# Threshold attention and a squared-ReLU layer: last keys padded with zeros, exponentials head by head, values between two parts of turning

## The chip, the cores and the metric

The kernel runs on one core of one Trainium2 chip. The metric is the device time of one execution in microseconds (us). A core has TensorE (PE), which multiplies matrices into PSUM, VectorE (DVE), ScalarE (ACT), GpSimd (POOL) and SyncE (SP, which here only issues DMAs). Each engine works through a queue of its own; semaphores order the engines among one another.

## The reference

Eight batches of eight heads attend over 576 tokens of 64 values. A score counts only if it lies within tau of its row's maximum. The result is laid out as 4608 tokens by 512 and goes through two matrix products with a squared ReLU between them.

```python
scores = scale * np.matmul(q, k.transpose(0, 1, 3, 2))      # scale = 1/8
thresh = np.max(scores, axis=-1, keepdims=True) - tau
scores = np.where(scores >= thresh, scores, -1000000000.0)
scores = scores - np.max(scores, axis=-1, keepdims=True)
attn = np.exp(scores)
attn = attn / (np.sum(attn, axis=-1, keepdims=True) + 1e-09)
attn_out = np.matmul(attn, v)                               # 8, 8, 576, 64
x = attn_out.transpose(0, 2, 1, 3).reshape(4608, 512)
h = x @ w_in                                                # 512 -> 2048
r = np.maximum(h, 0.0)
out = (r * r) @ w_out                                       # 2048 -> 512
```

Here q, k, v and the output are float32; the two weights come as float64, and the kernel rounds them to float32.

## The kernel before

**Visits and steps.** The kernel takes two heads at a time: a visit is one pair of heads with some of its blocks of 128 queries. 576 is four blocks of 128 and a rest of 64; the rests of the two heads make one block of 128 rows (block 4, the single-head block, since it needs one tile of scores in place of two). Visits 0 to 3 hold blocks 0 and 1 of the first batch's four pairs, visits 4 to 7 the blocks 2 to 4 of the same pairs, later visits all five. A step is one block of one visit. Steps 0 to 34 are visits 0 to 10, which turn the weights on PE ("early" below, though the kernel's own `early()` is true for steps 0 to 9 alone). From step 35 on (`by_dma`) DVE transposes 32x32 blocks and DMAs place them through DRAM. From visit 12 on (`paired`, `late_step`) visits go two by two.

**One early step** (the loop at L1082): `round_weights` stage 0, `scores` (L253: one PE product for each head and half of the keys, into banks 0 to 3; L268), `maxima` (L305, DVE), `turn(old, 0)` and `turn(old, 1)` for the block of two steps ago (L381: three PE transposes each, L388 for the single-head block; ACT copies them to `wT`, L382, L390), `exponents` (L314: on ACT the bias -max/8 at L317, the threshold max - 8 tau at L318, for both heads at once, then one exponential for each head, L320), `fill` with pieces of the MLP, `mix` (L493: the values of the block three steps ago, L496), its copy to `xT` (`put`, L479), `turn(old, 2)`, `threshold` (L323: DVE masks by comparing scores with the threshold and sums, L332, L334, L335), and `divide` (L337, POOL).

**Banks.** `take("tx", (4, 5))` deals PSUM banks 4 and 5 out in turn to the parts of turning and to the values; `take("mm", (6, 7))` deals 6 and 7 to MLP pieces, and to part 1 of turning while `early()` is true. A bank given out again waits until ACT has copied what it held.

**Rounding of weights.** The weights are rounded to float32 in 32 portions: stage 0 on ACT (L149, L150), 1 and 2 on DVE (L152, L154), 3 and 4 on POOL (L156, L158). Steps 2, 4 and 6 take one portion each, steps 8 to 33 one each, and steps 15, 18 and 22 two. Portion p + 3 is loaded after portion p is done.

**MLP pieces.** A piece is 8 or 4 products. `rate` spreads those at hand over the steps; each step has four calls of `fill`. Pieces are mlp_in (L544), mlp_out (L726) in the first chunk of 256 tokens, and from the third chunk on the seven-product scheme (L655, L761).

**The last keys.** `wT` holds the turned weights with keys on partitions. Keys 512 to 575 of head 0 lie on its partitions 0 to 63 and those of head 1 on 64 to 127, of one shared column block. In late visits the queries of the second group (`TWO`) have the two heads the other way round. The last keys' values are therefore loaded onto both halves of `vs`, and `mix` closes with products of 64 rows (`above`, `below`). `turn_blocks` (L406) writes each block's rest columns in one transpose for blocks 0 and 1 (L427), in two for blocks 2 and 3 (L429, L430).

**Order.** All five queues are in the order of the program (`manual_schedule`); nothing reorders them. `prep` (L227) transposes q and k of the next visit on DVE (L242) in a visit's last step.

Of the kernel before, what the change touches and what calls it, by code (L numbers as in the profile page):

```python
# [19 lines left out]
def kernel(  # L20
# [182 lines left out]
    def arrived(t):  # L203
        assert all(x[0].tensor.name != t.tensor.name for x in loads)

    def load_v(n):
        b, h = divmod(visits[n][0], HP)
        h *= 2
        t = vs[n % 2]
        if paired(n):  # L210
            both = t.rearrange("p (u c) d -> p u c d", u=2)
            src = v[b, h:h + 2]
            for u in range(2):
                loads.append((both[:, u, 0:NBLK, :], src[u, 0:NBLK * P, :].rearrange("(c p) d -> p c d", p=P)))
            for half in range(2):
                loads.append((both[half * D:(half + 1) * D, :, NBLK, :], src[:, NBLK * P:S, :].rearrange("u p d -> p u d")))
            return
        todo = []
        for u in range(2):
            at = u * (NBLK + 1)  # L220
            todo.append((t[:, at:at + NBLK, :], v[b, h + u, 0:NBLK * P, :].rearrange("(c p) d -> p c d", p=P)))
            for half in range(2):
                todo.append((t[half * D:(half + 1) * D, at + NBLK, :], v[b, h + u, NBLK * P:S, :]))
        for to, src in todo:
            nc.sync.dma_start(out=to, in_=src)

    def prep(n):  # L227

        prep_part(q, n)
        prep_part(k, n)  # L230
# [83 lines left out]
    def exponents(vis, i):  # L314
        w, sc, st = weights[vis, i]
        mx, thr, bias = (st[:, j, 0:len(sc)] for j in range(3))
        nc.scalar.activation(out=bias, in_=mx, func=AF.Copy, scale=-SCALE)  # L317
        nc.scalar.activation(out=thr, in_=mx, func=AF.Identity, bias=ntau8)  # L318
        for u in range(len(sc)):
            nc.scalar.activation(out=w[:, u, :].rearrange("p (h k) -> p h k", h=2), in_=sc[u],  # L320
                                 func=AF.Exp, bias=bias[:, u:u + 1], scale=SCALE)
# [84 lines left out]
    def turn_blocks(vis, i):  # L406
# [13 lines left out]
        if two:  # L420
            wb = wb[:, :, :, i % 2, :]
            whole_, rest_ = (w[:, :, x0 * 32:x1 * 32].rearrange("p u (c j q) -> p u c j q", q=32, j=n)
                             for x0, x1, n in ((0, M, 4), (M, KB, 2)))
            h = M // 4
            move(wb[:, 0:h, :, :], whole_[:, 0, :, :, :])  # L425
            if i < 2:
                move(wb[:, h, :, :].rearrange("p (u j) q -> p u j q", u=2), rest_[:, :, 0, :, :])  # L427
            else:
                move(wb[:, h, 2:4, :], rest_[:, 0, 0, :, :])  # L429
                move(wb[:, h, 0:2, :], rest_[:, 1, 0, :, :])  # L430
            move(wb[:, h + 1:, :, :], whole_[:, 1, :, :, :])  # L431
            return
        parts = [(0, 0, KB, 0), (1, M, KB, KB), (1, 0, M, KB + 2)] if paired(vis) else [(0, 0, KB, 2), (0, M, KB, 0)]
# [58 lines left out]

    def mix(n, cols):  # L493

        def term(ps, u, c, at, rows=slice(0, P), first=False, last=False):
            nc.tensor.matmul(ps[u * D:(u + 1) * D, :], vs[n % 2][rows, u * (NBLK + 1) + c, :],  # L496
                             wT[rows, at // REST:(at + ps.shape[1]) // REST, NBLK if c == NBLK else u * (NBLK + 1) + c, :],
                             start=first, stop=last)

        above, below = slice(0, D), slice(D, P)  # L500
        arrived(vs[n % 2])
        if not by_dma(n):
            ps = take("tx", (4, 5))[:, 0:cols.stop - cols.start]
            for c in range(NBLK):
                for u in range(2):
                    term(ps, u, c, cols.start, first=(c == 0))
            for u, rows in enumerate((above, below)):
                term(ps, u, NBLK, cols.start, rows, last=True)
            put(n, cols.start, ps, False)
            return  # L510
        n1, n2 = 2 * P + REST, 2 * P
        at = ODD if paired(n) and n % 2 else ONE
        one, two = bank[0], bank[4]
        groups = (one[:, 0:n1], at, (above, below)), (two[:, 0:n2], TWO, (below, above))
        for ps, x, _ in groups:
            for c in range(NBLK):
                for u in range(2):
                    term(ps, u, c, x, first=(c == 0))

        for ps, x, places in groups:  # L520
            for u, rows in enumerate(places):
                term(ps, u, NBLK, x, rows, last=True)
        put(n, 0, one[:, ONE - at:ONE - at + 2 * P], True)
        left = ODD if at == ODD else LEFT - at
        put(n, NBLK * P, one[:, left:left + REST], False)
        put(n, 2 * P, two[:, 0:n2], True)

# [292 lines left out]
    def by_dma(n):  # L822

        return n >= 3 * HP - 1
# [163 lines left out]
    make_identity(nc, ident)  # L988
    nc.gpsimd.dma_start(out=ntau8, in_=tau.to_broadcast([P, 1]))
    nc.gpsimd.memset(qmid, 0.0)  # L990
    for st in stats:
        nc.gpsimd.memset(st[:, 4, :], S * LITTLE)
    load_qk(1)
# [19 lines left out]
    def at_least(count, made):  # L1013
        while waiting and state["made"] < made + count:
            piece()

    def late_step(s):

# [63 lines left out]
    for s in range(END + 1):  # L1082
# [9 lines left out]
        if on:  # L1092
# [8 lines left out]
                load_qk(n + 2)  # L1101
            elif not short and at == 1 and not by_dma(n):
                load_qk(n + 1)
            if now:
                round_weights(now[0], 0)
            if s != 1:
                scores(s)
                after()
# [3 lines left out]
        lay = on and last and more and not by_dma(n) and s != 1  # L1112
        if old:
            turn(*old, 0)
            turn(*old, 1)
        if on:
            exponents(n, i)
            if s and by_dma(steps[s - 1][0]):
                turn_last(s)
            for p in now[1:]:  # L1120
                round_weights(p, 0)
            if at == 1:
                split_left(n)
            if lay:
                prep(n + 1)
            elif now:
                for p in now:
                    round_weights(p, 1)
        if s in mixes and not old:
            mix(*mixes[s])  # L1130
            for j in chunk_at.get(s, ()):
                add_chunk(j)
        quarter = rate(s) / 4 if s < END else 1e9
        fill(quarter)
        if s in mixes and old:
            mix(*mixes[s])
            for j in chunk_at.get(s, ()):
                add_chunk(j)
        if old:
            turn(*old, 2)  # L1140
        state["free"] = s > first_dma
# [8 lines left out]
        if on:  # L1150
            threshold(n, i)
            for fn in prep_at[s] + load_at[s]:
                fn()
            if lay and now:
                round_weights(now[0], 1)
            if now:
                round_weights(now[0], 2)
                round_weights(now[0], 3)
            for p in now[1:]:
                assert not lay  # L1160
                round_weights(p, 2)
                round_weights(p, 3)
            if not at_once:
                divide(n, i)
        if smooth:
# [59 lines left out]
```

## Time and profile before

| | |
|---|---|
| median of 3 runs | 1349.34 us (1346.12 to 1350.19) |
| profiled execution | 1348.74 us |
| its span, first to last instruction | 1346.9 us |
| mean granted PE clock | 0.992 |
| PE busy | 1305.0 us, 97% |
| PE weight loads busy | 1080.9 us, 80% |
| DVE busy | 925.7 us, 69% |
| ACT busy | 582.1 us, 43% |
| POOL busy | 760.4 us, 56% |
| part of PE in the chain that ended last | 83% |

The profile names instructions by engine, line and tiles; a float32 product shows as two records. Busy shares are means over stages with different limits, so the stages have to be read one by one. Idle time of an engine that does not set the end costs nothing. The ends of PE's records are modelled.

### The profile page before, as it was taken

Reading aid. Unit: us, or ns where it says so; the run is one execution under the profiler, and the core shown is the slowest. Engines: PE = TensorE matmul, PEld = TensorE weight load, DVE = VectorE, ACT = ScalarE, POOL = GpSimd, SP = SyncE. Lnnn points to the kernel's source line nnn. Section 1 sums busy time; section 2 is a strip of 40 time slices with the busy share of each in tenths; the row PEclk is TensorE's granted clock in tenths of the full one; section 3 lists DMA queues with packets and bytes.
Section 4 is the critical chain, followed back from the end, with each engine's and each line's share of the span. In section 5 each row is a group of like instructions: output and inputs, shape, how many; then the busy total and the mean of one; then the engine's idle time right before and its main releaser. Section 6 shows DMA issues by size and latency. Waiting matters only on the chain.

```text
span 1346.9 us, 25020 instructions
## 1 busy us (share of the span) xinstructions
PE 1305.0 (97%) x9112; PEld 1080.9 (80%) x9112; DVE 925.7 (69%) x2026; ACT 582.1 (43%) x1357; POOL 760.4 (56%) x861
## 2 busy tenths in 40 slices
PE   7899999989999999999999999999999999999998
PEld 5676556878787878878897888888897888889997
DVE  5877776868687777777778776868687877732231
ACT  4776674225253434435353435353435353522421
POOL 3679775754554646474638373737374737354451
PEclk7999999999999999999999999999999999999999
DMA  8764531738696777766786776768686676430000
GB/s 155 161 153 118 147 91 35 162 78 194 137 206 152 178 166 166 183 149 156 156 188 166 172 177 133 175 144 194 137 198 157 169 169 154 134 95 1 17 17 16
DMA packets 331883, 187.04 MB, mean 139 GB/s; under 512 B 293200, under 2 KB 293232, under 8 KB 325360
## 3 DMA queue, kind: packets, MB, share of 16 engines
q1 hardware_dynamic: 326656, 176.22, 56.5%
q0 software_dynamic: 2800, 8.93, 1.9%
q8 instruction: 72, 1.18, 0.4%
q10 hardware_dynamic: 2304, 0.29, 0.2%
q14 instruction: 51, 0.42, 0.1%
HBM read 109.58 MB, written 68.42 MB: 132 GB/s over the span
## 4 chain that ended last, share of the span: by engine, by line
PE 83%; DVE 5%; ACT 4%; DMA 4%; SPq 1%; POOL 1%; issue 1%; ACTq 0%; DVEq 0%; POOLq 0%
PE big L761 28%; PE big L655 26%; PE big L496 11%; PE big L284 8%; PE big L544 3%; PE big L268 3%; DMA aside<-turned 2%; PE big L726 2%; PE big L381 2%; DVE w L332 1%; ACT wT L382 1%; DMA wT<-aside 1%; ACT w L320 1%; DVE st L305 1%; PE big L261 0%
## 5 line engine op out<-in xcount | busy, mean ns | idle before, releaser
L305 DVE TENSOR_REDUCE st<-big 128x1 f32<-128x576 f32 x288 | 204.7, 750 | 137.7 <-PE big L284 101.8
L342 POOL TENSOR_SCALAR w<-w,st 128x576 f32<-128x576 f32 x269 | 253.6, 952 | 28.1 <-DVE st L335 24.1
L340 POOL TENSOR_SCALAR st<-st 128x2 f32<-128x2 f32 (+1 forms) x148 | 35.1, 237 | 372.9 <-DVE w L332 368.4
L761 PE MATMUL big<-wo,gsum 128*128 128x256 f32 x1088 | 244.9, 382 | 0.0
L761 PEld LDWEIGHTS big<-wo,gsum 128*128 128x128 f32 x1088 | 204.2, 190 | 38.4 <-issue 11.2
L332 DVE SCALAR_TENSOR_TENSOR w<-big,st,w 128x576 f32<-128x576 f32 x269 | 206.9, 805 | 35.1 <-ACT w L320 34.9
L761 PE MATMUL big<-wo,g 128*128 128x256 f32 x816 | 186.4, 382 | 0.0
L655 PE MATMUL big<-xT,w_in_sb 128*128 128x128 f32 x1536 | 185.6, 276 | 0.0
L320 ACT ACTIVATE w<-big,st 128x576 f32<-128x576 f32 x269 | 183.5, 733 | 0.0
L496 PE MATMUL big<-wT,vs 128*64 128x128 f32 (+7 forms) x1700 | 171.7, 361 | 11.3 <-ACT wT L382 4.0
L655 PEld LDWEIGHTS big<-xT,w_in_sb 128*128 128x128 f32 x1536 | 179.0, 192 | 3.8 <-issue 3.1
L761 PEld LDWEIGHTS big<-wo,g 128*128 128x128 f32 x816 | 151.2, 190 | 26.3 <-issue 7.2
L496 PEld LDWEIGHTS big<-wT,vs 128*64 128x64 f32 (+1 forms) x1700 | 98.2, 138 | 81.2 <-issue 26.0
L317 ACT ACTIVATE st<-st 128x2 f32<-128x2 f32 (+1 forms) x148 | 30.1, 204 | 256.8 <-DVE st L305 255.8
L667 DVE TENSOR_TENSOR g<-big,g 128x512 f32<-128x512 f32 x96 | 65.2, 681 | 87.4 <-PE big L655 83.1
L284 PE MATMUL big<-kT,qT 64*128 64x256 f32 (+3 forms) x768 | 108.8, 416 | 5.4 <-ACT seen L297 2.7
L284 PEld LDWEIGHTS big<-kT,qT 64*128 64x128 f32 x768 | 85.1, 186 | 21.9 <-issue 5.3
L425 DVE STREAM_TRANSPOSE turned<-w 128x512 f32<-128x512 f32 x100 | 70.3, 703 | 27.9 <-DMA aside<-turned 25.0
L534 POOL TENSOR_TENSOR gsum<-g 128x512 f32<-128x512 f32 x34 | 45.1, 1325 | 74.0 <-ACT g L664 68.2
L663 ACT ACTIVATE g<-g 128x512 f32<-128x512 f32 x96 | 60.2, 627 | 57.6 <-DVE g L667 57.6
L664 ACT ACTIVATE g<-g 128x512 f32<-128x512 f32 x128 | 80.7, 630 | 4.1
L431 DVE STREAM_TRANSPOSE turned<-w 128x512 f32<-128x512 f32 x100 | 66.9, 669 | 0.0
(112 smaller groups left out, 1965.8 us busy)
## 6 DMA issues: line engine op xcount, KB each, us to landing
aside<-turned SPq DMA_DIRECT2D x50, 1152.0 KB, 4.5
wT<-aside SPq DMA_DIRECT2D x200, 288.0 KB, 5.3
vs<-in_v_dram SPq DMA_DIRECT2D x72, 128.0 KB, 6.0
ql<-in_q_dram SPq DMA_DIRECT2D x126, 72.0 KB, 4.5
wo<-in_moe_w_in_dram SPq DMA_DIRECT2D x16, 512.0 KB, 4.5
wo<-in_moe_w_out_dram SPq DMA_DIRECT2D x16, 512.0 KB, 3.6
out_dram<-osb POOLq DMA_DIRECT2D x32, 256.0 KB, 3.5
kl<-in_k_dram SPq DMA_DIRECT2D x113, 72.0 KB, 3.2
```

The source lines that it names most:

```text
L284: nc.tensor.matmul(big[to, at + x0:at + x1], lhsT, keys[u * D:(u + 1) * D, x0:x1], start=True, stop=True)
L305: nc.vector.tensor_reduce(out=mx[:, u:u + 1], in_=sc[u], axis=AX.XY, op=ALU.max)
L320: nc.scalar.activation(out=w[:, u, :].rearrange("p (h k) -> p h k", h=2), in_=sc[u], func=AF.Exp, bias=bias[:, u:u + 1], scale=SCALE)
L332: nc.vector.scalar_tensor_tensor(out=wu, in0=sc[u], scalar=thr[:, u:u + 1], in1=wu, op0=ALU.is_ge, op1=ALU.mult, accum_out=sm[:, u:u + 1])
L342: nc.gpsimd.tensor_scalar(out=w[:, u, :], in0=w[:, u, :], scalar1=z[:, u:u + 1], scalar2=rcp[:, u:u + 1], op0=ALU.add, op1=ALU.mult)
L425: move(wb[:, 0:h, :, :], whole_[:, 0, :, :, :])
L431: move(wb[:, h + 1:, :, :], whole_[:, 1, :, :, :])
L496: nc.tensor.matmul(ps[u * D:(u + 1) * D, :], vs[n % 2][rows, u * (NBLK + 1) + c, :], wT[rows, at // REST:(at + ps.shape[1]) // REST, NBLK ...
L655: nc.tensor.matmul(to[:, f, :], factor(j, p, q, c)[:, f * P:(f + 1) * P], part[:, c, :], start=(p in "125" and f == 0 and c == 0), stop=(p ...
L664: nc.scalar.activation(out=to, in_=to, func=AF.Square)
L667: nc.vector.tensor_tensor(out=x, in0=to, in1=x, op=ALU.add)
L761: nc.tensor.matmul(to, left[:, f, :], wo[:, slot, f, :], start=(f == 0), stop=(f == HF - 1))
```

## The change

The last keys' values now lie only on one half of the partitions of `vs`, head 0's above and head 1's below; four memsets of POOL at the start put zeros on the other halves. `mix` multiplies all five column blocks over 128 rows, late visits group by group. `turn_blocks` writes the rest columns in one transpose for every block. In early steps the threshold is computed on DVE, and ACT computes bias and exponential of head 0, then bias and exponential of head 1. Rounding stage 0 comes after the exponentials, stages 1 to 3 after the masks. `mix` stands between parts 0 and 1 of turning, and part 1 after `mix`. The transpose of the next visit's k is moved from a visit's last step to the end of an earlier one (the first of a short visit, the fourth of a long one), after the rounding, except for visits 0 and 10 on.

```diff
--- before.py
+++ after.py
@@ -203,6 +203,11 @@
     def arrived(t):
         assert all(x[0].tensor.name != t.tensor.name for x in loads)
 
+    def last_keys(t, u, filled=True):
+
+        half = u if filled else 1 - u
+        return t[half * D:(half + 1) * D, u * (NBLK + 1) + NBLK, :]
+
     def load_v(n):
         b, h = divmod(visits[n][0], HP)
         h *= 2
@@ -212,15 +217,13 @@
             src = v[b, h:h + 2]
             for u in range(2):
                 loads.append((both[:, u, 0:NBLK, :], src[u, 0:NBLK * P, :].rearrange("(c p) d -> p c d", p=P)))
-            for half in range(2):
-                loads.append((both[half * D:(half + 1) * D, :, NBLK, :], src[:, NBLK * P:S, :].rearrange("u p d -> p u d")))
+                loads.append((last_keys(t, u), src[u, NBLK * P:S, :]))
             return
         todo = []
         for u in range(2):
             at = u * (NBLK + 1)
             todo.append((t[:, at:at + NBLK, :], v[b, h + u, 0:NBLK * P, :].rearrange("(c p) d -> p c d", p=P)))
-            for half in range(2):
-                todo.append((t[half * D:(half + 1) * D, at + NBLK, :], v[b, h + u, NBLK * P:S, :]))
+            todo.append((last_keys(t, u), v[b, h + u, NBLK * P:S, :]))
         for to, src in todo:
             nc.sync.dma_start(out=to, in_=src)
 
@@ -314,6 +317,13 @@
     def exponents(vis, i):
         w, sc, st = weights[vis, i]
         mx, thr, bias = (st[:, j, 0:len(sc)] for j in range(3))
+        if not by_dma(vis):
+            nc.vector.tensor_scalar(out=thr, in0=mx, scalar1=ntau8, scalar2=None, op0=ALU.add)
+            for u in range(len(sc)):
+                nc.scalar.activation(out=bias[:, u:u + 1], in_=mx[:, u:u + 1], func=AF.Copy, scale=-SCALE)
+                nc.scalar.activation(out=w[:, u, :].rearrange("p (h k) -> p h k", h=2), in_=sc[u],
+                                     func=AF.Exp, bias=bias[:, u:u + 1], scale=SCALE)
+            return
         nc.scalar.activation(out=bias, in_=mx, func=AF.Copy, scale=-SCALE)
         nc.scalar.activation(out=thr, in_=mx, func=AF.Identity, bias=ntau8)
         for u in range(len(sc)):
@@ -423,11 +433,7 @@
                              for x0, x1, n in ((0, M, 4), (M, KB, 2)))
             h = M // 4
             move(wb[:, 0:h, :, :], whole_[:, 0, :, :, :])
-            if i < 2:
-                move(wb[:, h, :, :].rearrange("p (u j) q -> p u j q", u=2), rest_[:, :, 0, :, :])
-            else:
-                move(wb[:, h, 2:4, :], rest_[:, 0, 0, :, :])
-                move(wb[:, h, 0:2, :], rest_[:, 1, 0, :, :])
+            move(wb[:, h, :, :].rearrange("p (u j) q -> p u j q", u=2), rest_[:, :, 0, :, :])
             move(wb[:, h + 1:, :, :], whole_[:, 1, :, :, :])
             return
         parts = [(0, 0, KB, 0), (1, M, KB, KB), (1, 0, M, KB + 2)] if paired(vis) else [(0, 0, KB, 2), (0, M, KB, 0)]
@@ -492,38 +498,27 @@
 
     def mix(n, cols):
 
-        def term(ps, u, c, at, rows=slice(0, P), first=False, last=False):
-            nc.tensor.matmul(ps[u * D:(u + 1) * D, :], vs[n % 2][rows, u * (NBLK + 1) + c, :],
-                             wT[rows, at // REST:(at + ps.shape[1]) // REST, NBLK if c == NBLK else u * (NBLK + 1) + c, :],
-                             start=first, stop=last)
-
-        above, below = slice(0, D), slice(D, P)
+        def terms(ps, at):
+            for c in range(NBLK + 1):
+                for u in range(2):
+                    nc.tensor.matmul(ps[u * D:(u + 1) * D, :], vs[n % 2][:, u * (NBLK + 1) + c, :],
+                                     wT[:, at // REST:(at + ps.shape[1]) // REST, NBLK if c == NBLK else u * (NBLK + 1) + c, :],
+                                     start=(c == 0), stop=(c == NBLK))
+
         arrived(vs[n % 2])
         if not by_dma(n):
             ps = take("tx", (4, 5))[:, 0:cols.stop - cols.start]
-            for c in range(NBLK):
-                for u in range(2):
-                    term(ps, u, c, cols.start, first=(c == 0))
-            for u, rows in enumerate((above, below)):
-                term(ps, u, NBLK, cols.start, rows, last=True)
+            terms(ps, cols.start)
             put(n, cols.start, ps, False)
             return
-        n1, n2 = 2 * P + REST, 2 * P
         at = ODD if paired(n) and n % 2 else ONE
         one, two = bank[0], bank[4]
-        groups = (one[:, 0:n1], at, (above, below)), (two[:, 0:n2], TWO, (below, above))
-        for ps, x, _ in groups:
-            for c in range(NBLK):
-                for u in range(2):
-                    term(ps, u, c, x, first=(c == 0))
-
-        for ps, x, places in groups:
-            for u, rows in enumerate(places):
-                term(ps, u, NBLK, x, rows, last=True)
+        terms(one[:, 0:2 * P + REST], at)
+        terms(two[:, 0:2 * P], TWO)
         put(n, 0, one[:, ONE - at:ONE - at + 2 * P], True)
         left = ODD if at == ODD else LEFT - at
         put(n, NBLK * P, one[:, left:left + REST], False)
-        put(n, 2 * P, two[:, 0:n2], True)
+        put(n, 2 * P, two[:, 0:2 * P], True)
 
 
 
@@ -988,6 +983,9 @@
     make_identity(nc, ident)
     nc.gpsimd.dma_start(out=ntau8, in_=tau.to_broadcast([P, 1]))
     nc.gpsimd.memset(qmid, 0.0)
+    for t in vs:
+        for u in range(2):
+            nc.gpsimd.memset(last_keys(t, u, False), 0.0)
     for st in stats:
         nc.gpsimd.memset(st[:, 4, :], S * LITTLE)
     load_qk(1)
@@ -1013,6 +1011,10 @@
     def at_least(count, made):
         while waiting and state["made"] < made + count:
             piece()
+
+    def at_once_k(n):
+
+        return 0 < n and not by_dma(n + 1)
 
     def late_step(s):
 
@@ -1101,8 +1103,6 @@
                 load_qk(n + 2)
             elif not short and at == 1 and not by_dma(n):
                 load_qk(n + 1)
-            if now:
-                round_weights(now[0], 0)
             if s != 1:
                 scores(s)
                 after()
@@ -1112,30 +1112,26 @@
         lay = on and last and more and not by_dma(n) and s != 1
         if old:
             turn(*old, 0)
-            turn(*old, 1)
         if on:
             exponents(n, i)
             if s and by_dma(steps[s - 1][0]):
                 turn_last(s)
-            for p in now[1:]:
+            for p in now:
                 round_weights(p, 0)
             if at == 1:
                 split_left(n)
             if lay:
-                prep(n + 1)
-            elif now:
-                for p in now:
-                    round_weights(p, 1)
-        if s in mixes and not old:
+                prep_part(q, n + 1)
+                if not at_once_k(n):
+                    prep_part(k, n + 1)
+        if s in mixes:
             mix(*mixes[s])
             for j in chunk_at.get(s, ()):
                 add_chunk(j)
+        if old:
+            turn(*old, 1)
         quarter = rate(s) / 4 if s < END else 1e9
         fill(quarter)
-        if s in mixes and old:
-            mix(*mixes[s])
-            for j in chunk_at.get(s, ()):
-                add_chunk(j)
         if old:
             turn(*old, 2)
         state["free"] = s > first_dma
@@ -1151,15 +1147,11 @@
             threshold(n, i)
             for fn in prep_at[s] + load_at[s]:
                 fn()
-            if lay and now:
-                round_weights(now[0], 1)
-            if now:
-                round_weights(now[0], 2)
-                round_weights(now[0], 3)
-            for p in now[1:]:
-                assert not lay
-                round_weights(p, 2)
-                round_weights(p, 3)
+            for p in now:
+                for stage in (1, 2, 3):
+                    round_weights(p, stage)
+            if at == (0 if short else 3) and more and at_once_k(n):
+                prep_part(k, n + 1)
             if not at_once:
                 divide(n, i)
         if smooth:
```

## The prediction

> **What bounds the kernel now.** I read the slices of the page first, then busy time by stage, then PE's waits, then single steps in the timeline. Busy time by stage (columns: stretch, its length, then busy time and instructions of PE, PE's weight loads, DVE, ACT, POOL, then clock, DMA share, GB/s):
>
> ```profile
> 8.00:61.00 53.00, 44.03 (x292) 31.34 (x292) 41.29 (x96) 32.77 (x81) 25.79 (x35) 0.87 0.74 157
> 61.00:213.00 152.00, 142.52 (x1101) 97.61 (x1103) 113.89 (x252) 109.09 (x270) 124.07 (x134) 1.00 0.48 124
> 213.00:600.00 387.00, 371.26 (x2496) 304.15 (x2497) 287.30 (x638) 148.10 (x356) 215.93 (x247) 0.99 0.67 153
> 600.00:1347.00 747.00, 742.67 (x5208) 643.67 (x5206) 482.10 (x1042) 290.83 (x652) 391.78 (x434) 1.00 0.56 134
> ```
>
> From 600 us PE is never idle. In 61 to 213 us, which is steps 10 to 34, PE idles only 9.5 of 152 us. So the span is PE's work plus PE's gaps, and any gap added in the early steps is added to the end, since PE has no slack later in which to give it back. What PE waits for between 60 and 215 us (waiter, released by, total us, times, longest):
>
> ```profile
> PE big L496 <- ACT wT L382: 4.0, 11, 1.4
> PE big L496 <- ACT wT L390: 1.6, 4, 0.4
> PE big L261 <- DVE w L332: 1.2, 1, 1.2
> PE big L261 <- ACT wT L395: 0.9, 1, 0.9
> PE big L261 <- ACT qmid L237: 0.7, 1, 0.7
> ```
>
> The values (L496) wait for the copy out of part 0 (L382, L390), because both use bank 4 or 5. One typical step, 28, from the timeline (start, length, engine, line; x counts records, two to a float32 product):
>
> ```profile
> 175.62 1.24 PE L268 MATMUL big<-kT,qT 64*128 64x288 f32 x8
> 176.79 0.87 PE L381 MATMUL big<-ident,w 128*128 128x128 f32 x6
> 176.89 1.42 DVE L305 TENSOR_REDUCE st<-big 128x1 f32<-128x576 f32 x2 [2.02 <-PE big L268]
> 177.37 0.86 ACT L382 COPY wT<-big 128x384 f32<-128x384 f32 x2 [1.75 <-PE big L381]
> 177.90 1.46 PE L496 MATMUL big<-wT,vs 128*64 128x128 f32 x20 [0.24 <-ACT wT L382]
> 178.34 0.20 ACT L317 ACTIVATE st<-st 128x2 f32<-128x2 f32 x1
> 178.64 1.35 ACT L320 ACTIVATE wo<-big,st 128x576 f32<-128x576 f32 x2
> 179.29 0.55 PE L381 MATMUL big<-ident,w 128*128 128x128 f32 x3
> 179.40 0.82 DVE L332 SCALAR_TENSOR_TENSOR wo<-big,st,wo 128x576 f32<-128x576 f32 x1 [0.75 <-ACT wo L320]
> 179.89 0.26 ACT L479 COPY xT<-big 128x128 f32<-128x128 f32 x1
> 180.40 0.70 ACT L149 ACTIVATE turned<-wo 128x512 f32<-128x512 f32 x1
> ```
>
> PE goes scores, two parts of turning, values, last part, an MLP piece, next scores at 181.40, with 0.24 us of gap. The copy of the values (L479) comes after the exponentials, and nothing on PE waits for it. The rounding (L149) follows.
>
> [...] L479 starts at 179.89 although the values ended near 179.3; the exponentials stood ahead. [...]
>
> **The change part by part.** Durations are start to start where instructions overlap.
>
> *1. The last keys in late values (25 visits).* Before, these four half-height products run at once on four quarters:
>
> ```profile
> 412.05 0.60 PE L496 MATMUL big<-wT,vs 128*64 128x256 f32 x4
> 413.01 0.49 PE L496 MATMUL big<-wT,vs 64*64 64x320 f32 x4
> 413.29 0.48 PE L496 MATMUL big<-wT,vs 64*64 64x256 f32 x4
> 413.70 0.48 PE L761 MATMUL big<-wo,g 128*128 128x256 f32 x1
> ```
>
> They take 413.01 to 413.70, 0.69[...]. After, they are two full-height pairs: two records of 0.27 (320 columns) and two of 0.215 (256) make 0.97. Difference +0.19 to +0.28, I take 0.22: 25 x 0.22 = +5.5 us, all on a saturated PE. It also saves one DVE transpose in each of 50 blocks (0.202 + 0.204 becomes 0.270: 6.8 us of DVE), which I cost at nothing: DVE is busy 482 of 747 us there. Values loads: four issues a visit instead of four or six, fewer bytes, hidden by SP. POOL's four 64x64 memsets at the start (0.1 to 0.22 each, by the other memsets) end before any value is used. Early values: five pairs either way, no cost.
>
> *2. Values between parts 0 and 1; roundings behind the exponentials: steps 10 to 33.* Banks 4 and 5 are dealt in turn. Before: part 0 A, part 1 B, values A, part 2 B. After: part 0 A, values B, part 1 A, part 2 B. So **part 2 now waits for the copy of the values**, and ACT's queue has that copy behind part 0's copy, both exponentials and, newly, the rounding's two activations. In the built order every part 2 of steps 10 to 33 carries this wait. Behind part 2 on PE stand the step's remaining MLP pieces and the next scores, and for these DVE and ACT wait.
>
> Clock of such a step, from the scores at 0: scores end 1.18, part 0 1.62, values 3.0, part 1 3.45: PE stands at part 2. ACT: copy of part 0 1.76 to 2.19 (in step 30, 188.77 against 187.01); bias and exponential of head 0 (0.25 + 0.69) to 3.14, head 1 to 4.1; rounding 0.58 + 0.57 to 5.25; copy of the values to 5.52; PE goes on at 5.6. **Gap 2.15 us.** Variants: a piece between parts 1 and 2 (1.75) leaves 0.4; a single-head step reaches part 2 at 2.8 or 3.25 and is released at 4.5; two qmid copies ahead of the values' copy add 0.5; a second rounding 1.2; values of 64 columns, 0.44 less work ahead; parts of the single-head block are 0.2 shorter and their copy 0.15 earlier. By the built order:
> - two heads, no piece ahead, steps 12, 22, 23, 25 to 28: 2.9 + 3.8 + 2.15 + 2.15 + 2.9 + 2.6 + 2.15 = 18.65
> - one head, steps 10, 13, 16, 19, 24, 29: 3 x 1.25 + 3 x 1.7 = 8.85
> - turning the single-head block, a piece ahead, steps 15, 18 (two roundings), 21, 31: 2 x 2.35 + 2 x 1.15 = 7.0
> - two heads, a piece ahead, steps 11, 14, 17, 20, 30, 32, 33: 6 x 0.4 + 0.85 = 3.25
>
> Sum 37.75. Against it, the 9.5 us of present gaps nearly all go (values no longer wait for L382/L390; waits by L261 are covered): I take 9.2. Net **+28.5 us**. With slower steps DVE (masks to 5.0, rounding to 6.25, transpose of k to 7.0; next maxima at 7.3) and POOL do not bind.
>
> *3. Head by head, k's transpose moved: steps 0 to 9.* Here part 1 uses banks 6/7, so part 2 has no new wait. The loop now is 5.19 us (mask 40.12, scores, maxima 41.39, bias 43.35, exponential 43.66, mask 44.44, scores 45.31). The bias need not wait for the second maximum or part 1's copy: 0.45 less. But DVE takes on the threshold sum (0.11 as L998 to 0.17 as L335), and rounding (0.9) and k's transpose (0.73) stand after the masks in one step of two, ahead of the next maxima, out of the ACT wait (1.14 at 44.44) that hid L152. A pair of steps on DVE: maxima 2.9, thresholds 0.3, masks 3.2, sums 0.8, rounding 0.9, transposes 1.5 = 9.6, plus a wait of 1.05 for the first exponential: 10.65 against 10.4. Five pairs +1, the first steps (16 to 30 us), where the chain is longer, -1.5: **-0.5**, bounds -3 to +4.
>
> Sum: 28.5 + 5.5 - 0.5 = +33.5. Span 1346.9 becomes 1380.4; with 1.84 outside it 1382.2 against this execution's 1348.74; that lay 0.6 below the median, so 1383.
>
> **Rivals.** *Faster:* the exponential chain sets steps 0 to 33, and head by head takes 0.45 off each: -15 + 5.5, about 1340. For it: the loop at 40 to 45 us closes through the bias. Against: from step 10 PE has 9.5 us of gaps to give, and the new wait is in the program. It decides if the copy of the values is done about when PE reaches part 2: with gaps below 4 us in all (0.17 a step), the sum is no longer slower. *Half:* ACT is ahead of my clock (exponentials start before part 0's copy costs them, less bias latency) and gaps are half: 18.9 - 9.2 + 5.5 - 0.5, 1364. *Last keys alone:* early stalls equal the gaps that go: 1354. *Worse:* rounded weights come later, so pieces and weight loads wait (ACT L150 already waited twice 3 us for POOL L158): ten more, 1393.
>
> **How the numbers follow.** Main case 0.74, worse 0.10, half 0.09, last keys alone 0.03, faster 0.04. Main case's own bounds: gaps 30 to 45, late 3 to 8, early -3 to +4: 1368 to 1395. The range reaches to the half case: 1362 to 1394. What a measurement can tell from no change is 0.3%, 4 us: faster 0.03, same 0.04 (the 1354 case lies at its edge), slower 0.93.
>
> **What would show it.** Right: PE's part 2 waits for ACT's copy xT, 30 to 45 us in total within 60 to 250 us, about 2 us where no piece stands ahead; the wait of the values for L382/L390 gone; PE's gaps in steps 10 to 33 near 38; the late values 4.9 to 5.0 us instead of 4.72, without 64*64 records; steps 4 to 9 still 5.1 to 5.4 apart. Wrong: dense stage starting (first L284) at about the old 260 us, or steps 22 to 28 of under 7 us.

## The result, and the profile after

The changed kernel takes 1388.28 us (median of 4 runs, 1385.5 to 1392.5), the kernel before 1348.26 us beside it (4 runs, 1346.12 to 1350.19). The ratio is 1.0301, with a 95% interval of 1.0279 to 1.0323: 3% slower. The prediction was 1383 us, with a range of 1362 to 1394.

The profiled execution of the changed kernel took 1385.5 us, its span is 1383.7. Where the 36.8 us between the two spans lie follows from the starts of the first scores of step 10 and of step 35 in the two timelines:

| stretch | before | after | difference | predicted |
|---|---|---|---|---|
| start to step 10 | 61.06 | 62.71 | +1.65 | -0.5 |
| steps 10 to 34 | 151.76 | 185.24 | +33.5 | +28.5 |
| step 35 to the end | 1134.1 | 1135.75 | +1.65 | +5.5 |
| span | 1346.9 | 1383.7 | +36.8 | +33.5 |

Busy time by stage of the changed kernel (columns as before: stretch, length, busy time and instructions of PE, PE's weight loads, DVE, ACT and POOL, clock, DMA share, GB/s):

```profile
62.70:247.90 185.20, 152.71 (x1099) 103.07 (x1099) 117.59 (x271) 110.63 (x263) 119.02 (x133) 0.94 0.39 99
247.90:1383.70 1135.80, 1117.88 (x7701) 956.62 (x7701) 767.07 (x1630) 440.26 (x1006) 608.00 (x680) 1.00 0.59 139
```

The kernel before, cut at the same steps:

```profile
61.00:212.80 151.80, 142.35 (x1099) 97.44 (x1099) 113.73 (x250) 108.89 (x270) 123.87 (x134) 1.00 0.48 124
212.80:1346.90 1134.10, 1114.11 (x7701) 947.99 (x7701) 769.57 (x1680) 439.13 (x1007) 607.91 (x680) 1.00 0.60 140
```

In steps 10 to 34 PE runs 1099 records in both kernels. Its gaps grow from 9.45 us (151.80 - 142.35) to 32.49 (185.20 - 152.71), which is +23.0. And its busy time grows by 10.4 us, with the clock at 0.94 in place of 1.00. Those two make the 33.4 us. From step 35 on PE is busy 3.8 us longer and idles 2.1 us less.

What PE waits for between 60 and 250 us in the changed kernel (waiter, released by, total us, times, longest):

```profile
PE big L391 <- ACT xT L485: 20.9, 17, 3.6
PE big L404 <- ACT xT L485: 10.9, 6, 2.7
PE big L264 <- ACT qmid L240: 2.2, 1, 2.2
PE big L271 <- DVE wo L342: 0.6, 1, 0.6
```

31.8 of the 32.5 us of gaps in steps 10 to 34 are part 2 of turning (L391, and L404 for the single-head block) waiting for ACT's copy of the values (L485, before L479). The old waits of the values (now L504) for the copies of turning are gone. (The qmid wait stands just ahead of step 10.) Step 28 of the changed kernel in the timeline, PE and ACT alone (start, length, engine, line):

```profile
204.12 1.24 PE L271 MATMUL big<-kT,qT 64*128 64x288 f32 x8
205.29 0.55 PE L391 MATMUL big<-ident,w 128*128 128x128 f32 x3
205.78 1.31 PE L504 MATMUL big<-wT,vs 128*64 128x128 f32 x20
205.88 0.48 ACT L392 COPY wT<-big 128x384 f32<-128x384 f32 x1 [4.04 <-PE big L391]
...
207.02 0.55 PE L391 MATMUL big<-ident,w 128*128 128x128 f32 x3
...
207.48 0.74 ACT L324 ACTIVATE wo<-big,st 128x576 f32<-128x576 f32 x1
208.12 0.65 ACT L149 ACTIVATE turned<-wo 128x512 f32<-128x512 f32 x1
208.67 0.66 ACT L150 ACTIVATE turned<-wo 128x512 f32<-128x512 uint32 x1
209.22 0.26 ACT L485 COPY xT<-big 128x128 f32<-128x128 f32 x1
209.36 0.50 ACT L392 COPY wT<-big 128x384 f32<-128x384 f32 x1
209.53 0.55 PE L391 MATMUL big<-ident,w 128*128 128x128 f32 x3 [1.97 <-ACT xT L485]
```

PE has done part 1 at 207.57 and stands until 209.53. ACT is never idle in that time: exponentials, the two activations of the rounding, and only then the copy of the values that frees the bank. Part 1's copy, behind it at 209.36, is not what PE waits for.

The clock is the part that the prediction did not have. Windows of 3.41 us around that wait and the one before it (columns as above):

```profile
196.69:200.10 3.41, 1.25 (x24) 0.95 (x23) 2.93 (x8) 3.18 (x7) 0.00 (x0) 1.00 0.01 2
200.10:203.51 3.41, 3.09 (x6) 1.71 (x7) 1.06 (x4) 1.13 (x4) 1.96 (x3) 0.50 0.45 154
206.93:210.34 3.41, 1.44 (x11) 0.89 (x8) 2.96 (x10) 3.06 (x8) 0.00 (x0) 1.00 0.01 2
210.34:213.75 3.41, 3.41 (x6) 1.68 (x5) 0.62 (x1) 0.25 (x1) 3.16 (x5) 0.50 0.46 151
```

PE idles 2.16 and 1.97 us in the first and third; in the window after each its clock is 0.50 throughout. Six such slow windows fall on this execution between 60 and 250 us, at 63.6, 84.1, 107.9, 159.1, 200.1 and 210.3. At half clock each loses 3.41 / 2 = 1.71 us: 10.2 us, about the growth of PE's busy time. The rest of that time is the same only in sum: without the slow windows, the values take 28.0 us in place of 31.1 in these steps, scores 27.4 in place of 28.5, and turning, whose parts now end at a gap, 31.8 in place of 26.9. The kernel before has no slow window in this stage.

The late values, between two pieces of the seven-product scheme:

```profile
465.11 5.07 PE L504 MATMUL big<-wT,vs 128*64 128x320 f32 x40
470.11 1.13 PE L756 MATMUL big<-wo,gsum 128*128 128x256 f32 x4
```

From their start to the next product they take 5.00 us in all but 2 of the 25 visits, 4.72 us before; the 64x64 records are gone.

### The profile page after: what moved, and what is told of

It is laid out like the page before. It is cut to its first block, busy times and chain, and to the rows that moved or that the text cites. A ratio compares the mean times of both kernels' runs of the same rounds, so it can differ in the third digit from the quotient of the medians.

```text
span 1383.7 us, 25048 instructions
## 1 busy us (share of the span) xinstructions
PE 1318.6 (95%) x9112; PEld 1095.4 (79%) x9112; DVE 932.2 (67%) x2011; ACT 585.6 (42%) x1350; POOL 757.1 (55%) x865
## 4 chain that ended last, share of the span: by engine, by line
PE 79%; ACT 8%; DVE 4%; SPq 4%; DMA 4%; issue 2%; POOL 0%; DVEq 0%; ACTq 0%; POOLq 0%
PE big L756 27%; PE big L650 26%; PE big L504 9%; PE big L287 7%; PE big L539 3%; PE big L271 2%; SPq L458 2%; PE big L721 2%; ACT w L324 2%; PE big L391 1%; DMA aside<-turned 1%; ACT turned L149 1%; ACT turned L150 1%; DVE st L308 1%; DVE w L342 1%
## 5 line engine op out<-in xcount | busy, mean ns | idle before, releaser
L504 PE MATMUL big<-wT,vs 128*64 128x128 f32 (+3 forms) x1700 | 171.9, 354 | 4.7 <-DVE w L342 2.9
L504 PEld LDWEIGHTS big<-wT,vs 128*64 128x64 f32 x1700 | 107.7, 139 | 61.8 <-issue 12.3
L330 ACT ACTIVATE w<-big,st 128x576 f32<-128x576 f32 x225 | 153.5, 733 | 0.0
L327 ACT ACTIVATE st<-st 128x2 f32<-128x2 f32 (+1 forms) x113 | 22.8, 202 | 246.0 <-DVE st L308 245.8
L435 DVE STREAM_TRANSPOSE turned<-w 128x512 f32<-128x512 f32 x100 | 70.3, 703 | 27.6 <-DMA aside<-turned 24.6
L156 POOL TENSOR_TENSOR turned<-turned 128x512 f32<-128x512 f32 x32 | 40.7, 1271 | 77.6 <-DVE turned L154 70.4
```

Of the source, the lines that this page charges most:

```text
L504: nc.tensor.matmul(ps[u * D:(u + 1) * D, :], vs[n % 2][:, u * (NBLK + 1) + c, :], wT[:, at // REST:(at + ps.shape[1]) // REST, NBLK if c = ...
```

## The experiments

The theory after the result: the time is the wait for the bank that the values hold; how long it lasts is set by what ACT has ahead of the copy of the values; and the slow clock follows from the gaps. The main rivals: the later roundings and masks hold PE up in some other way; the load, not the idling, lowers the clock. Each experiment's time is set against the kernel before on the same chip: 1347.03 us (35 runs) for the old order of the values, the copy ahead of the rounding, the last keys alone and head by head alone, 1346.39 us (42 runs) for the other four.

**The old order of the values, all else changed.**

```diff
         if old:
             turn(*old, 0)
+            turn(*old, 1)
...
-        if s in mixes:
+        if s in mixes and not old:
             mix(*mixes[s])
...
-        if old:
-            turn(*old, 1)
         fill(quarter)
+        if s in mixes and old:
+            mix(*mixes[s])
...
```

> The changed kernel with the old order of turning and values put back (parts 0 and 1, exponentials, pieces, values, part 2); all other parts of the change stay. If part 2's wait for the copy of the values, with the clock that falls in its gaps, is what makes steps 10 to 34 33 us longer, those gaps go, PE's clock is 1.00 there, and the time falls from 1388 to about 1352 to 1358. If it is the roundings behind exponentials and masks that hold the early steps up, whatever the order of the values, it stays above 1375.

Measured: 1354.43 us, ratio 1.0053 (1.0034 to 1.0073). Steps 10 to 34 take 151.1 us, as before the change (151.8):

```profile
63.94:215.03 151.09, 141.78 (x1100) 98.66 (x1100) 127.34 (x272) 108.01 (x262) 119.12 (x132) 0.98 0.48 122
```

So all that steps 10 to 34 lost comes with the order of the values. Under the old order, the roundings behind the exponentials, the thresholds on DVE and k's moved transpose cost these steps nothing in sum. The clock is 0.98 there, not the 1.00 expected. Two slow windows follow waits behind ACT (scores for the qmid copy at 63.9 us, mlp_out for its input at 145.2), and cheaper values (see the last keys below) make up for them.

**The copy of the values ahead of the rounding on ACT.** The changed kernel with stage 0 of the rounding behind `mix`.

```diff
             exponents(n, i)
-            for p in now:
-                round_weights(p, 0)
...
         if s in mixes:
             mix(*mixes[s])
...
+        for p in now:
+            round_weights(p, 0)
         if old:
             turn(*old, 1)
```

> The changed kernel with the rounding's two ScalarE activations moved behind the copy of the values; the values still lie between parts 0 and 1, in the same banks. If the wait is for a copy that stands behind the rounding, each gap is 1.15 us shorter (2.4 with two roundings): gaps of about 2.1 fall to about 1.0, those behind a piece vanish, in all 8 to 12 us instead of 32, PE's clock does not fall, and the time is 1355 to 1362. If the order of the values alone costs the time, with the rounding only a bystander, it stays above 1378.

Measured: 1359.99 us, ratio 1.0094 (1.0074 to 1.0115); steps 10 to 34 take 159.2 us. Its waits of PE between 60 and 240 us:

```profile
PE big L391 <- ACT xT L485: 8.8, 9, 1.5
PE big L404 <- ACT xT L485: 3.5, 3, 1.6
```

Steps 10 to 34 in the view by stage:

```profile
60.43:219.64 159.21, 144.83 (x1100) 99.83 (x1100) 130.57 (x276) 110.26 (x265) 120.42 (x133) 0.98 0.46 116
```

The waits come to 12.3 us in place of 31.8. Of the 33.5 us lost in these steps, 26 hang on two activations, 0.55 us each from start to start, that stand ahead of one copy in every step with a rounding. Of the remaining 7.4 us, 4.9 are longer gaps, in which the exponentials still stand ahead of the copy, and the rest is the clock. It was expected not to fall, but two slow windows, at 122.8 and 170.6 us, cost 3.4, of which cheaper values (see the last keys below) give a part back.

**The bank alone.** In steps 10 to 33 the values go into the last 128 columns of the bank that part 1 then fills (part 1 has 384 of the 512; for the single-head block its four tiles of 64 columns are packed into 256), so that part 2 gets part 0's bank, copied long before. Order on PE and roundings stay as changed. On ACT the copy of the values now stands behind that of part 1. No run here has it ahead, while PE still writes part 1 into the same bank.

```diff
+        if part == 1 and used.get("tail") is not None:
+            ps = used["tail"]
+            used["tail"] = None
...
-            ps = take("tx", (4, 5))[:, 0:cols.stop - cols.start]
+            ps = take("tx", (4, 5))
+            if tail:
+                used["tail"] = ps
+            ps = ps[:, 3 * P:][:, 0:cols.stop - cols.start] if tail else ps[:, 0:cols.stop - cols.start]
...
+            return lambda: put(n, cols.start, ps, False)
...
         if old:
             turn(*old, 1)
+        if then:
+            then()
```

> The changed kernel, same order on every engine but two copies: in steps 10 to 33 the values go into the last 128 columns of the bank that part 1 of turning then fills, so that part 2 gets the bank of part 0, which is copied early; the copy of the values stands behind that of part 1 on ACT. Theory (the lost time is the wait for the bank, and the slower clock follows from it): waits of part 2 for the copy of the values fall from 31.8 us to under 3, PE's clock in steps 10 to 34 is back at 0.98 to 1.00, these steps take 143 to 153 us instead of 185, the time is 1343 to 1353 us. Rival (the roundings and masks behind the exponentials delay the weights themselves, so that the stall only turns into waits of the values or of the next scores): 1360 to 1385 us.

Measured: 1348.59 us, ratio 1.0011 (1.0002 to 1.0019). Its steps 10 to 34 and its stage from step 35 on, in the view by stage:

```profile
62.48:209.08 146.60, 139.90 (x1100) 99.21 (x1100) 131.94 (x272) 108.75 (x263) 119.64 (x132) 1.00 0.48 125
209.08:1347.00 1137.92, 1121.17 (x7701) 958.87 (x7701) 767.63 (x1630) 440.12 (x1006) 608.99 (x681) 1.00 0.59 139
```

Its waits of PE between 60 and 250 us that are longest in sum:

```profile
PE big L271 <- DVE wo L342: 4.9, 4, 1.8
PE big L264 <- ACT qmid L240: 2.5, 3, 1.9
PE big L545 <- ACT osb L733: 1.1, 1, 1.1
PE big L395 <- ACT xT L489: 0.7, 1, 0.7
```

With nothing changed but the bank and two copies, 38.6 of the 185.2 us go, one wait of 0.7 us for xT is left of 31.8, and the clock is 1.00. The rival that the late roundings hold PE up by themselves is out. What remains in their place is small: scores that wait for masks (4.9 us), now that PE is early. The stage is 5.2 us shorter than in the kernel before; 1.4 us more ahead of step 10 and 3.8 more from step 35 on take that back. This late stage has two slow windows, as before the change, and PE's busy time there is 7.06 us above the 1114.11 of before: the last keys' own price in the late values.

**Work in the gap.** The transposes of part 1 are issued four times over, into the same place, in those of steps 10 to 33 in which no piece stands ahead of part 2.

```diff
-            for n in range(3):
+            for n in list(range(3)) * (1 + again):
...
+        piece_next = waiting and state["left"] + quarter >= PIECE_US / 2 and waiting[0][0] <= state["usable"]
         if old:
-            turn(*old, 1)
+            turn(*old, 1, 0 if piece_next or early() or s not in mixes else 3)
```

> The changed kernel, but in those of steps 10 to 33 in which no piece stands ahead of part 2 the transposes of part 1 are issued four times over, into the same place: 1.3 us more of PE work that nobody needs, put into the gap of about 2.2 us. Theory (PE's clock falls because PE idles for 2 us and more): the gaps left are under 1.5 us, the clock in steps 10 to 34 is 0.98 or more instead of 0.94, PE's needed work there shrinks by 7 to 10 us, the time falls to 1376 to 1382 us although PE does more. Rival (the clock falls for another reason, such as the load of the steps): clock still 0.93 to 0.95, time 1386 to 1392 us.

Measured: 1382.16 us, ratio 1.0264 (1.0243 to 1.0286). Steps 10 to 34:

```profile
61.80:243.30 181.50, 160.70 (x1233) 113.53 (x1233) 117.47 (x272) 110.18 (x262) 119.20 (x133) 0.97 0.40 101
```

PE does 134 records more and the stage is 3.7 us shorter. There are three slow windows between 60 and 250 us in place of six. The clock is 0.97, not 0.98, and the time stands just above what the theory gave: gaps of 1.8 to 2.0 us are left in four steps, those that turn the single-head block, and one of 2.6 in a step with two roundings. The three slow windows that stay, at 61.5, 105.9 and 157.1 us, follow gaps that stayed long: the qmid wait ahead of step 10 (2.24 us) and two of the gaps just named (1.96 and 2.62). Those that fell away stood behind gaps that became shorter: 2.73 to 2.00 us in step 12, 2.48 to 1.50 in step 27, 1.97 to 0.99 in step 28. This kernel and the changed one were not timed side by side, and the same gaps can give more or fewer slow windows from one execution to the next (below), so the size of the gain is rough. What it shows is that more load on PE did not slow the clock: 0.97 with 1233 records of PE in these steps, 0.94 with 1099.

**The last keys alone.** The kernel before with the zero-padded values, `mix` over 128 rows and the single transpose of the rest columns; nothing else.

```diff
+                loads.append((last_keys(t, u), src[u, NBLK * P:S, :]))
...
+        terms(one[:, 0:2 * P + REST], at)
+        terms(two[:, 0:2 * P], TWO)
```

> The kernel before with the zero-padded last keys alone (loads, memsets, values over 128 rows, one transpose for the rest columns). By the records of both kernels the late values take 5.00 us instead of 4.715: 25 times 0.285 is 7 us on a PE that is never idle, so 1353 to 1356. The rival is what the late stage of the changed kernel showed, only 1.5 us longer in all: then 1349 to 1351, and something gives 5 us back.

Measured: 1348.52 us, ratio 1.0011 (1.0004 to 1.0018), 1.5 us above the kernel before. The rival was right. The values do take 5.00 us here too, 7.1 us over 25 visits, and three things give most of it back:

```profile
61.39:211.96 150.57, 139.83 (x1099) 97.20 (x1099) 114.00 (x251) 108.70 (x269) 124.08 (x134) 1.00 0.47 121
211.96:1347.70 1135.74, 1119.00 (x7701) 958.15 (x7701) 767.88 (x1630) 440.34 (x1007) 608.30 (x680) 1.00 0.59 139
```

First, the early values became cheaper. The last two of their ten products ran on 64 rows each before, and now all have 128; the 20 records of step 28 take 1.31 us in place of 1.46. In steps 10 to 34 the values take 28.0 us of PE in place of 31.1, so PE is busy 139.83 us instead of 142.35. Second, PE idles less from step 35 on, 16.7 us instead of 20.0. The five other runs with the new last keys, and the changed kernel, have 16.5 to 17.9 us there, while the two other runs with the old ones have 19.4 and 19.6. Which part of the change does that, such as the DVE transpose saved in each block, was not tested apart. Third, in the profiled execution one slow window did not fall. The wait for the placed weights near 580 us, 2.05 us here, lies 0.7 in one clock window and 1.3 in the next, where the kernel before had its 2.6 us in one window.

**Head by head alone.** The kernel before with the new `exponents`.

```diff
+        if not by_dma(vis):
+            nc.vector.tensor_scalar(out=thr, in0=mx, scalar1=ntau8, scalar2=None, op0=ALU.add)
+            for u in range(len(sc)):
+                nc.scalar.activation(out=bias[:, u:u + 1], in_=mx[:, u:u + 1], func=AF.Copy, scale=-SCALE)
+                nc.scalar.activation(out=w[:, u, :].rearrange("p (h k) -> p h k", h=2), in_=sc[u],
+                                     func=AF.Exp, bias=bias[:, u:u + 1], scale=SCALE)
+            return
```

> The kernel before with the exponentials head by head and the threshold on VectorE alone, in early steps. If the loop through bias and exponential sets steps 2 to 9, and PE sets the steps after, this takes 0.2 to 0.45 off eight steps: 1344 to 1347, the odd steps as in the changed kernel. If VectorE's threshold or the copies ahead of the bias take it back, no change: 1348 within 1.

Measured: 1349.35 us, ratio 1.0014 (1.0003 to 1.0026), a little above both expectations. Steps 5 to 8 are 5.38 us apart, 5.20 before. The exponential that starts earlier brings nothing. DVE is next in the loop and carries the threshold now, 0.23 us in the median, which is about what each step grew by; that this is the reason was not tested apart.

**k's transpose back in a visit's last step.**

```diff
     def at_once_k(n):
-        return 0 < n and not by_dma(n + 1)
+        return False
```

> The changed kernel with the transpose of the next visit's k where it was before, in a visit's last step beside that of q, ahead of the masks. Theory (in steps 4 to 9 it lengthens every second step because it stands, with the rounding, between the masks and the next maxima): the pair of steps of 4.8 and 6.15 us comes to 10.2 to 10.6 us, steps 2 to 9 take 44 to 45.3 us instead of 46.5, the time is 1385 to 1387.5 us. Rival (DVE's work is the same, so the pair is): 10.9 to 11.1 us, time unchanged within 1 us or, from steps 10 on, up to 3 us longer.

Measured: 1385.15 us, ratio 1.0286 (1.0264 to 1.0308), not told apart from the changed kernel's 1.0301. In the trace the pair of steps 6 and 7 takes 4.82 + 5.79 = 10.61 us, against 4.82 + 6.15 = 10.97 with the transpose moved, and steps 2 to 9 take 45.56 us in place of 46.52. Both are just above what the theory gave. So the moved transpose costs about 0.35 us in this pair of early steps.

This run shows one thing more. From step 10 on it has the same waits for xT (32.0 us in all, against 31.8), yet steps 10 to 34 take 190.1 us in place of 185.2. It has nine slow windows between 60 and 250 us, not six. Three times 1.71 is 5.1. Of its four runs the profiled one is the slowest, with a mean clock of 0.983; the fastest, 1382.62 us, has 0.989.

**The shared bank in the kernel before.** Values between parts 0 and 1 in steps 10 to 33, sharing part 1's bank; last keys, exponentials, roundings and k's transpose as before.

```diff
         if old:
             turn(*old, 0)
-            turn(*old, 1)
+            if early() or s not in mixes:
+                turn(*old, 1)
...
+        if s in mixes and not (old and early()):
+            then = mix(*mixes[s], bool(old) and not by_dma(mixes[s][0]))
...
+            if old:
+                turn(*old, 1)
+            if then:
+                then()
         quarter = rate(s) / 4 if s < END else 1e9
```

> The kernel before, but in steps 10 to 33 the values stand between parts 0 and 1 of turning and share the bank of part 1, as in the experiment on the shared bank; last keys, exponentials, roundings and k's transpose are as before. Theory (PE is the bound, and 5.6 of its 9.5 us of gaps there are the wait of the values for part 0's or part 1's copy): the values no longer wait, steps 10 to 34 take 144 to 148 us instead of 151.8, the time is 1340 to 1345 us. Rival (in these steps DVE or ACT set the pace and the gap moves to the next scores): 1346 to 1351 us.

Measured: 1343.52 us (22 runs), ratio 0.9985 (0.9976 to 0.9993): faster than the kernel before by 0.15%. That is less than the 0.3% which the prediction set for a few runs; 22 runs against 42 resolve it, and the interval excludes no change. Its steps 10 to 34:

```profile
59.65:208.03 148.38, 143.72 (x1099) 99.46 (x1099) 116.84 (x251) 107.45 (x269) 123.97 (x134) 1.00 0.51 131
```

Its waits of PE between 60 and 250 us that are longest in sum:

```profile
PE big L268 <- DVE wo L332: 4.7, 5, 1.2
PE big L550 <- ACT osb L738: 1.1, 1, 1.1
PE big L261 <- ACT qmid L237: 0.7, 1, 0.7
```

The values wait no more, and the gaps are 4.7 us in place of 9.45. 3.4 us are gained in the stage, not the 4 to 8 expected: scores now wait for masks, as in the other run with this bank, and PE is busy 1.4 us longer. Both of the expectations hold in part. So the order that the change chose is a little better than the old one, if the bank does not make part 2 wait.

## Why the prediction was right, and where it was off

**What bounds the kernel.** Right. The gaps that part 2 got in steps 10 to 33 stayed in the span: with the bank shared, 38.6 us went from the stage and 36.7 from the span.

**Part 2's wait.** The mechanism and its place are right, as the runs with the old order and with the other bank show. The sizes, by the prediction's classes:

| class | predicted | measured |
|---|---|---|
| two heads, no piece ahead (7 steps) | 18.65 | 17.2 |
| one head (6 steps) | 8.85 | 7.0 |
| turning the single-head block, a piece ahead (4) | 7.0 | 5.4 |
| two heads, a piece ahead (7) | 3.25 | 2.2 |
| sum | 37.75 | 31.8 |

Step 28 followed its clock within 0.2 us: first exponential 2.44 us after the scores' start (predicted 2.44), rounding 4.00 (4.1), copy of the values 5.10 (5.25), PE on at 5.41 (5.6). The small excess in most steps makes the 6 us, with step 10, counted at 1.25, which has no wait. The present gaps went as said, so the gaps grew by 23.0, not 28.5.

**The clock.** The sum has no term for it, and that is its largest miss: +10.2 us between 60 and 250 us. All durations in the working were taken at full clock, and the prediction never asked what idling does to the clock. The near agreement of +33.5 with +36.8 is thus partly luck, two errors that cancel: gaps 5.5 too many, clock 10.2 too few. The profiled execution is also the fastest of the four; between the medians the change costs 40.0 us.

**Last keys.** The change in each visit was put at 0.22 us, with bounds of 0.19 to 0.28; it is 5.00 - 4.715 = 0.285, so 7.1 us and not 5.5. That is the upper bound, 0.97 - 0.69. The lower one also took as saved that the first half-height product starts 0.31 us after the last 128x64 one (412.70 to 413.01, against 0.215 between pairs of 256 columns): about 0.09. It was not saved: after the change the last values and the next product start 0.31 us apart (469.80 and 470.11). What makes these steps longer was not shown. The run with the shared bank confirms the 7.1 (7.06 of PE busy time). In the stage this was hidden: two slow windows of the kernel before (at 278 and 582 us, in and behind gaps of 2.7 and 2.6 us) did not fall in the changed kernel, -3.4, and gaps were 2.1 us less. 7.1 - 3.4 - 2.1 = +1.6, as measured.

Two terms that the prediction put at nothing were not nothing. "Early values: five pairs either way, no cost": they take 3.1 us less of PE in steps 10 to 34, in every run with the new last keys. In the changed kernel this brings nothing, since PE then waits for the copy; with the shared bank it does. And what the last keys save on DVE was put at nothing, but PE idles less from step 35 on in all of these runs.

**Early steps.** -0.5 was taken, +1.65 came, inside the bounds. Steps 2 to 8 together fit, 39.6 us against 39.7 before; but single steps from 4 to 9 take 4.1 to 6.9 us, long and short in turn, where 5.1 to 5.4 was to be the sign. The miss is one wait that the prediction had called covered ("waits by L261 are covered"):

```profile
61.06 0.66 ACT L149 ACTIVATE turned<-wo 128x512 f32<-128x512 f32 x1
61.61 0.66 ACT L150 ACTIVATE turned<-wo 128x512 f32<-128x512 uint32 x1
62.17 0.48 ACT L240 COPY qmid<-qT 64x64 f32<-64x64 f32 x2
...
62.71 1.49 PE L264 MATMUL big<-kT,qmid 128*128 128x288 f32 x4 [2.23 <-ACT qmid L240]
```

The scores of step 10 are the first of a single-head block. They wait 2.23 us for its queries' copy, which stands behind the rounding on ACT; before, they waited 0.7. With the rounding behind the values the wait is 1.1 us and step 9 takes 5.11 us, against 6.92 in the changed kernel and 5.34 before. It is the same mistake in small as the main effect is in large: a copy that PE needs, behind a rounding that PE does not need yet.

**The rivals.** *Faster* fell with the heads-alone run. *Half* and *last keys alone* assumed small gaps. *Worse* assumed pieces waiting for late roundings; no such wait is among PE's. Its time, 1393, lies close to the slowest run, 1392.5, but for another reason: the slow windows.

## What to carry to other kernels

When two users take turns at a few banks, moving one of them in the order decides whose copy the next one waits for; so list for each bank which copy frees it, and what stands ahead of that copy on its engine. Keep ahead of such a copy nothing that can wait: two activations of 0.55 us each, ahead of one copy in each of some 24 steps, cost 26 us here. And price a gap on PE at more than its length: where PE idled about 2 us in one clock window, 1.7 us at half clock came on top, six times in the changed kernel between 60 and 250 us. Last, when a bank is shared by several users, see whether two of them fit into it together: the values in the free columns of part 1's bank took the wait away.

## What the runs showed of the hardware

In these traces the slow stretches of PE's clock lie on a grid. In the changed kernel the six between 60 and 250 us start at 63.57, 84.05, 107.94, 159.14, 200.10 and 210.34 us, and each has a clock of 0.50 for 3.41 us. The distances are 20.48, 23.89, 51.20, 40.96 and 10.24 us: 6, 7, 15, 12 and 3 times 3.413 us within 0.02 (146.77 us in all, over 43 windows). Ahead of the six, PE idled 1.95 to 2.73 us of a window's 3.41. PE's idle time in each window of this grid, worked out from the starts and lengths of its records, longest first, for the changed kernel between 60 and 250 us:

```
idle in the window, us    2.73  2.67  2.23  2.15  1.96  1.95  1.81  1.57  1.56  1.48
clock in the next window  0.50  0.50  0.50  0.50  0.50  0.50  1.00  1.00  1.00  1.00
```

The same count in the windows at full clock from about 48 to 260 us, for the changed kernel, the copy ahead of the rounding, work in the gap and k's transpose back: each of the 17 windows with 1.84 us or more of idling was followed by a slow one, and none with under 1.46. Between those it went both ways (1.46 twice, 1.54, 1.62 and 1.64 slow; 1.48, 1.49, 1.55 to 1.58, 1.69, 1.73, 1.79 and 1.81 not), so idle time alone, as far as these records show it, does not decide. What else counts was not shown.

The grid does not start with the kernel: the slow window behind the gap ahead of step 10 starts 0.86 us after the scores of that step in the changed kernel, 1.40 after them with k's transpose back, and 0.30 before them with work in the gap. So the same gap may lie in one window or be split by two. A wait of 2.75 us at 188.4 us was split (1.48 and 1.26) and did no harm, while one of 1.96 us inside a single window cost 1.71 more. This fits the run with k's transpose back, which has nearly the same gaps and nine slow windows, not six. It also fits the spread of the changed kernel's four runs: 1385.5, 1386.6, 1390.0 and 1392.5 us, with mean clocks of 0.988, 0.985, 0.984 and 0.980. Where the windows lay in the three runs that have no trace is not known.
